# A fused S5 scan and sliding-window attention kernel rebuilt around frames of two steps, with rotation matrices on VectorE and GpSimd left idle

## The chip, the cores and the metric

The kernel runs on one core of a Trainium2 chip. The core has five engines that run side by side and meet through semaphores: PE (TensorE, the matrix engine), DVE (VectorE), ACT (ScalarE), POOL (GpSimd) and SP (SyncE, which issues most of the transfers here). PEld is PE's weight load, which overlaps PE. SBUF is the on-chip memory; PSUM holds what PE produces, and copying a PSUM tile to SBUF is called an eviction here.

The metric is device time in microseconds (us); lower is better. A ratio is the mean time of one kernel's fast runs over that of the kernel before in the same rounds on the same chip, so it is not quite the ratio of the medians quoted beside it. Where I write a difference in microseconds between two variants, it is the difference of their ratios times 212.0 us, a typical median of the kernel before in these rounds. A compile-time scheduler re-sorts each engine's instructions after every edit, so I do not read effects below about 1% (2 us) as causes unless the trace shows them too.

## The reference

Two independent parts run over 2048 positions of width 448 in bf16; the result is their concatenation, 2048 x 896.

```python
# Part A: S5, a diagonal complex recurrence with 448 states
dt = exp(log_dt); Lam_bar = exp(dt * Lam)                 # Lam = Lambda_re + i Lambda_im
B_bar = ((Lam_bar - 1) / Lam)[:, None] * (B_re + 1j*B_im)
h[t] = Lam_bar * h[t-1] + B_bar @ x[t]
y[t] = 2 * Re(C @ h[t]) + Dskip * x[t]

# Part B: attention, 16 heads of 28, window of 8 keys, dilation 2
q, k, v = split(x @ wqkv)
logits[s, w] = q[s] . k[s - 2w] / sqrt(28)     # -1e9 where s - 2w < 0
o[s] = sum_w softmax_w(logits)[s, w] * v[s - 2w]
out = o @ wo
```

Both kernels put 128 chunks of 16 consecutive positions on the 128 partitions, so that "position j" means 128 rows, one from each chunk. Attention needs 14 positions of the chunk before: the halo, which is copied by DMA; the first chunk's halo is zero. PE makes the projections. The logits and the weighted sum of v are elementwise products and sums on VectorE, because each position has its own keys. In part A, multiplying a state by a power of Lam_bar is a 2x2 rotation, which PE applies as a sparse 128x128 "rotation matrix"; these are built on the chip from the parameters.

## The kernel before

The order of the calls is: B's projections, A's weights and scan, then B's attention last.

```python
    b.prep(); a.setup(); b.qk_proj(); b.v_proj()
    a.setup_c(); a.setup_weights(); b.loads2()
    a.main()
    b.attention()
```

`prep` loads x whole, permutes the qkv weights with VectorE copies, and fills the first halo with zeros by DMA:

```python
        nc.sync.dma_start(self.x_sb[:], self.B_x[0].rearrange("(p j) d -> p j d", j=T))
        # ... (prep)
        V.tensor_copy(wpv[:, :, 0:2], wnv[:, :, 0:2])
        V.tensor_copy(wpv[:, :, 2], wnv[:, :, 2])
        # ... 16 transposes of x_sb, evicted by ScalarE
        nc.sync.dma_start(t_[0:1, :, 0:HALO, :]...)      # zeros, for kd and vd
```

The logits and the product with v use one temporary each (`qd`, `kd`, `vd` hold all 16 positions):

```python
        for w in range(W):                        # attention
            V.tensor_tensor(pr[:], qd[:]..., kd[:, :, off:off + T, :]..., op=ALU.mult)
            V.tensor_tensor(pr[:, 0:14], pr[:, 0:14], pr[:, 14:28], op=ALU.add)
            # ... four more halvings, the last into fp32 logits
        # ... softmax in fp32
        for (j0, j1) in self.PV_SPLIT:            # ((0, 12), (12, 16))
            for w in range(W):
                # ...
                tmp = pool.tile([NCH, DH, T, H], bf16, name="pv_tmp", tag="prod")   # one buffer
                V.tensor_tensor(tmp[:, :, 0:n, :], aa, vv, op=ALU.mult)
                V.tensor_tensor(acc[:, :, j0:j1, :], acc[:, :, j0:j1, :], tmp[:, :, 0:n, :], op=ALU.add)
            self.tail(j0, j1)       # transpose, VectorE eviction, wo product, ScalarE eviction, store
```

Part A builds its matrices on GpSimd (`build_mats(..., G)`), steps through 16 positions, and sends every local state through DRAM and back (`hs`) until the carried-in state is known:

```python
        for j in range(T):
            ht = self._level1_step(j, (lambda m: prev_t[:, m, :]), j > 0)   # 128-column products
            nc.sync.dma_start(hs[j], ht[:]...)
        # ... seven scan steps over the 128 chunks
        for j in range(T):
            nc.sync.dma_start(hin[:]..., hs[j])
            # ... hin + rotation of the carried-in state; then y = C h + Dskip x
```

## Time and profile before

The kernel before takes 211.73 us (median of 3 runs, 211.53 to 213.08). The profiled run spans 211.4 us.

| what | before | view |
|---|---|---|
| VectorE busy | 181.0 us, 86% | page, part 1 |
| PE busy | 160.4 us, 76% | page, part 1 |
| PE columns streamed | 335,040, about 141 us at 448 columns per 0.189 us | counted from the matmul records |
| first product on PE | 18.5 us | list of waits |
| VectorE idle in the first 20 us | 11.1 us | table by stretches |
| VectorE idle from there to its last instruction | 14.5 us | table by stretches and timeline |
| after VectorE's last instruction | 4.8 us | timeline |

These are lines of the page of the kernel before: the busy time of each engine with its share and its instructions; the busy tenths of PE and VectorE in 40 slices of 5.3 us; and the shares of the chain of work that ended last.

```profile
PE 160.4 (76%) x1709; PEld 117.4 (56%) x1709; DVE 181.0 (86%) x197; ACT 100.2 (47%) x193; POOL 28.1 (13%) x35
PE   0004999999997799999995763998888883297773
DVE  0359998888929999999999996999999999999950
PE 46%; DVE 33%; ACT 8%; DMA 6%; issue 3%; SPq 2%; ACTq 0%; DVEq 0%
```

VectorE is busy from slice 4 to slice 38, with dips at slices 12 and 25. PE does nothing for three slices, and it has holes while attention ends the kernel. One line of the list of waits says why nothing starts (waiter, its tile, what released it, us in total, times, longest):

```profile
PE pt_x L80 <- DMA xb_sb<-in_B_x_dram: 18.5, 1, 18.5
```

The table by stretches gives, after the stretch and its length, the busy us and the instructions of PE, PEld, DVE, ACT and POOL, then PE's clock, the DMA share and GB/s. Before:

```profile
0.00:20.00 20.00, 1.22 (x10) 1.12 (x11) 8.90 (x30) 5.37 (x12) 1.15 (x19) 1.00 0.66 184
110.00:141.00 31.00, 21.02 (x238) 15.68 (x236) 28.07 (x27) 19.74 (x36) 0.00 (x0) 0.89 0.16 49
141.00:204.00 63.00, 46.77 (x413) 30.05 (x412) 61.68 (x43) 23.77 (x49) 0.00 (x0) 0.92 0.28 83
```

In the last of these stretches VectorE is busy for 61.68 us of 63: there the kernel waits for VectorE. The groups by shape show what it does (line, engine, operation, output and input, shape and type, count, busy us, mean ns, idle before); the last one is a GpSimd matrix:

```profile
L129 DVE TENSOR_TENSOR prod<-qd,kd 128x7168 bf16<-128x7168 bf16 x8 | 30.7, 3840 | 0.1
L165 DVE TENSOR_TENSOR pv_tmp<-attn,vd 128x5376 bf16<-128x5376 bf16 x7 | 20.7, 2957 | 0.2
L167 DVE TENSOR_TENSOR acc<-acc,pv_tmp 128x5376 bf16<-128x5376 bf16 x6 | 17.7, 2957 | 0.2
L343 POOL TENSOR_TENSOR Mmat<-Dm,Scat 128x896 bf16<-128x896 f32 x7 | 11.6, 1688 | 19.3 <-DVE Scat L335 19.3
```

Two pairs from the timeline (start, length, engine, line, operation): in the first, a copy of 7 elements in each partition lasts as long as the GpSimd product beside it; in the second, a product and its sum follow one another.

```profile
23.26 3.19 POOL L343 TENSOR_TENSOR Lmat<-Dm,Shl 128x1792 bf16<-128x1792 f32 x1 [0.61 <-DVE Shl L340]
23.30 3.17 DVE L327 COPY sB<-g_im 64x7 f32<-64x7 f32 x1
...
147.73 2.96 DVE L165 TENSOR_TENSOR pv_tmp<-attn,vd 128x5376 bf16<-128x5376 bf16 x1
150.72 2.96 DVE L167 TENSOR_TENSOR acc<-acc,pv_tmp 128x5376 bf16<-128x5376 bf16 x1
```

### The profile page before, as it was taken

To read this page: it belongs to the slowest core of one execution; us is meant where nothing else is said; L and a number is where in the kernel's file an instruction comes from. 1 tells how busy PE (TensorE), PEld (TensorE's weight loads), DVE (VectorE), ACT (ScalarE), POOL (GpSimd) and SP (SyncE) were. 2 spreads that over 40 slices of the span, in tenths; PEclk is the share of its full clock that TensorE was granted. 3 is DMA by queue.
4 is the path that set the end of the run, shared out by engine and by line. 5 is a ranking of instruction groups with operands and counts; after the bars stand their busy time and mean duration, and the time that the engine had idled before them with its cause. 6 is when DMAs were issued, how large, how long until landed. Compare 5 with 4: busy or idle time off the path is not lost.

```text
span 211.4 us, 4117 instructions
## 1 busy us (share of the span) xinstructions
PE 160.4 (76%) x1709; PEld 117.4 (56%) x1709; DVE 181.0 (86%) x197; ACT 100.2 (47%) x193; POOL 28.1 (13%) x35
## 2 busy tenths in 40 slices
PE   0004999999997799999995763998888883297773
PEld 0003765555567799999994652565555551154441
DVE  0359998888929999999999996999999999999950
ACT  2053792002689993344337796344455541024432
POOL 2000899991000000000000000000000000000000
PEclk9999999999999999999999998599999999569999
DMA  1599940485508515422231011134354411012212
GB/s 0 103 351 289 244 108 0 108 192 161 212 2 209 95 47 171 164 106 90 87 118 59 3 43 43 47 110 129 92 137 126 112 43 43 0 43 72 83 65 87
DMA packets 23836, 22.17 MB, mean 105 GB/s; under 512 B 11786, under 2 KB 23114, under 8 KB 23562
## 3 DMA queue, kind: packets, MB, share of 16 engines
q1 hardware_dynamic: 20231, 20.32, 32.9%
q10 hardware_dynamic: 3587, 1.59, 3.2%
q8 instruction: 13, 0.21, 0.5%
q14 instruction: 5, 0.04, 0.1%
HBM read 11.36 MB, written 7.34 MB: 88 GB/s over the span
## 4 chain that ended last, share of the span: by engine, by line
PE 46%; DVE 33%; ACT 8%; DMA 6%; issue 3%; SPq 2%; ACTq 0%; DVEq 0%
PE qkv_ps L95 18%; DVE pv_tmp L165 13%; DVE acc L167 10%; PE l1A L392 7%; DMA xb_sb<-in_B_x_dram 6%; PE l1B L392 5%; PE wo_ps L188 3%; PE pt_x L80 3%; DVE oT_sb L185 2%; PE pt_x L415 2%; DVE o_nat L169 2%; ACT Bcat L379 2%; PE l1A L397 1%; PE l1A L399 1%; ACT Ccat L250 1%
## 5 line engine op out<-in xcount | busy, mean ns | idle before, releaser
L95 PE MATMUL qkv_ps<-wqkv_p,xbT_sb 112*128 112x448 bf16 x192 | 40.1, 361 | 0.0
L129 DVE TENSOR_TENSOR prod<-qd,kd 128x7168 bf16<-128x7168 bf16 x8 | 30.7, 3840 | 0.1
L165 DVE TENSOR_TENSOR pv_tmp<-attn,vd 128x5376 bf16<-128x5376 bf16 (+1 forms) x14 | 28.3, 2021 | 0.3
L95 PEld LDWEIGHTS <-xbT_sb 112*128 112x128 bf16 x192 | 18.8, 100 | 15.5
L392 PEld LDWEIGHTS <-Bcat 112*128 112x128 bf16 x448 | 26.2, 98 | 0.0
L167 DVE TENSOR_TENSOR acc<-acc,pv_tmp 128x5376 bf16<-128x5376 bf16 (+1 forms) x12 | 24.3, 2024 | 0.3
L80 PE MATMUL pt_x<-ident,xb_sb 128*112 128x128 bf16 x64 | 7.8, 266 | 18.8 <-DMA xb_sb<-in_B_x_dram 18.5
L483 ACT CAST ya<-y_ps 128x448 bf16<-128x448 f32 x16 | 8.5, 531 | 23.4 <-issue 18.8
L191 ACT CAST yb<-wo_ps 128x448 bf16<-128x448 f32 x16 | 8.5, 532 | 23.3 <-PE wo_ps L188 23.3
L80 PEld LDWEIGHTS <-xb_sb 128*112 128x112 bf16 x64 | 7.5, 173 | 21.1 <-DMA xb_sb<-in_B_x_dram 18.5
L402 ACT CAST ht<-l1A 128x512 bf16<-128x512 f32 x16 | 9.4, 587 | 19.2 <-issue 17.0
L119 ACT CAST vd<-qkv_ps 128x448 bf16<-128x448 f32 x16 | 8.4, 536 | 20.8 <-PE qkv_ps L95 20.7
L392 PE MATMUL l1A<-xaT_sb,Bcat 112*128 112x128 bf16 x256 | 18.1, 219 | 0.0
L188 PE MATMUL wo_ps<-wo_p,oT_sb 112*128 112x448 bf16 x64 | 15.0, 382 | 3.8 <-DVE oT_sb L185 3.7
L131 DVE TENSOR_TENSOR prod<-prod 128x3584 bf16<-128x3584 bf16 x8 | 16.2, 2025 | 0.3
L343 POOL TENSOR_TENSOR Mmat<-Dm,Scat 128x896 bf16<-128x896 f32 x7 | 11.6, 1688 | 19.3 <-DVE Scat L335 19.3
L392 PE MATMUL l1B<-xaT_sb,Bcat 112*128 112x128 bf16 x192 | 14.2, 219 | 0.0
L81 ACT COPY xbT_sb<-pt_x 112x512 bf16<-112x512 bf16 x16 | 8.8, 587 | 7.3 <-PE pt_x L80 7.3
L184 PE MATMUL pt_o<-ident,o_nat 128*112 128x128 bf16 x64 | 5.8, 244 | 8.3 <-DVE o_nat L169 8.3
L113 DVE TENSOR_SCALAR qd<-qkv_ps 128x448 bf16<-128x448 f32 x16 | 10.0, 625 | 2.1
L188 PEld LDWEIGHTS <-oT_sb 112*128 112x128 bf16 x64 | 6.0, 103 | 10.1 <-DVE oT_sb L185 5.0
L469 PEld LDWEIGHTS <-ident 128*128 128x128 bf16 x112 | 11.3, 101 | 0.0
(206 smaller groups left out, 360.9 us busy)
## 6 DMA issues: line engine op xcount, KB each, us to landing
hs<-ht SPq DMA_DIRECT2D x16, 224.0 KB, 1.9
hin<-hs SPq DMA_DIRECT2D x16, 224.0 KB, 2.7
xb_sb<-in_B_x_dram SPq DMA_DIRECT2D x1, 1792.0 KB, 12.3
xa_sb<-in_A_x_dram SPq DMA_DIRECT2D x1, 1792.0 KB, 7.9
out_dram<-ya SPq DMA_DIRECT2D x16, 112.0 KB, 1.7
out_dram<-yb SPq DMA_DIRECT2D x16, 112.0 KB, 1.7
kd<-kd ACTq DMA_DIRECT2D x1, 1372.0 KB, 9.1
vd<-vd SPq DMA_DIRECT2D x1, 1372.0 KB, 9.4
```

Source lines behind the costliest of these rows:

```text
L80: nc.tensor.transpose(pt[:, k, :], self.x_sb[:, j, k * KP:(k + 1) * KP], self.ident[:])
L95: nc.tensor.matmul(ps[:].rearrange("p d h -> p (d h)"), lhsT=self.xT[:, k, j, :], rhs=self.wp[:, k * 3 + which].rearrange("p d h -> p (d h)"),
L113: V.tensor_scalar(self.qd[:, :, j, :], ps[:], scale, None, op0=ALU.mult)
L129: V.tensor_tensor(pr[:], qd[:].rearrange("p d j h -> p d (j h)"), kd[:, :, off:off + T, :].rearrange("p d j h -> p d (j h)"), op=ALU.mult)
L131: V.tensor_tensor(pr[:, 0:14], pr[:, 0:14], pr[:, 14:28], op=ALU.add)
L165: V.tensor_tensor(tmp[:, :, 0:n, :], aa, vv, op=ALU.mult)
L167: V.tensor_tensor(acc[:, :, j0:j1, :], acc[:, :, j0:j1, :], tmp[:, :, 0:n, :], op=ALU.add)
L188: nc.tensor.matmul(ps[:], lhsT=oT[:, kt, j, :], rhs=self.wo_p[:, kt, :], start=(kt == 0), stop=(kt == KT - 1))
L343: eng.tensor_tensor(out_tile, Dm[:].unsqueeze(1).unsqueeze(1).to_broadcast([NCH, n, 2, PL]), scal.unsqueeze(3).to_broadcast([NCH, n, 2, PL ...
L392: nc.tensor.matmul(reg(m), lhsT=self.Bcat[:, k, m, :], rhs=self.xT[:, k, j, :], start=(k == 0 and m in (0, MA)), stop=(not has_prev and k ...
L402: nc.scalar.copy(ht[:, 0:MA, :], psA[:])
L469: nc.tensor.matmul(reg(m), lhsT=ident[:], rhs=hin[:, m, :], start=(m in (0, MA)), stop=False, skip_group_check=True)
```

## The change

The intent is to take work off VectorE, to keep PE fed from the start to the end, and to keep GpSimd out of VectorE's way. Nearly every line is rewritten, so the diff is cut to its core here, in the order of the kernel, with "..." at the cuts and comments of mine.

```diff
+    def warm(self, n, mode="full"):            # products of zeros while PE would wait
+            if mode == "full":
+                mm(wp[0][:, 0:NCH], lhsT=z[:, 0:NCH], rhs=z[:, 0:NCH], start=True, stop=True)
+            elif mode == "cols":                # 32 columns of the array at a time
+            else:                               # "rows": 64 rows of the array at a time
 ...
-        nc.sync.dma_start(self.x_sb[:], self.B_x[0].rearrange("(p j) d -> p j d", j=T))
+        self.nc.sync.dma_start(self.x_sb[:, j0:j1, :], xv[:, j0:j1, :])     # five pieces, w in thirds
-        V.tensor_copy(wpv[:, :, 0:2], wnv[:, :, 0:2])
-        V.tensor_copy(wpv[:, :, 2], wnv[:, :, 2])
+        pv = ps[:].rearrange("p (h d) -> p d h", h=H)      # the permutation is done by the eviction
 ...
-        for w in range(W):                                  # logits: all 16 positions, one prod buffer
+    def qk(self, hf):                                       # logits: 8 positions, two pr buffers
+            V.tensor_tensor(pr[:].rearrange("p d j h -> p j d h"), self.q[hf][:], self.kd[:, off:off + HJ], op=ALU.mult)
+            V.tensor_tensor(pr[:, 0:14], pr[:, 0:14], pr[:, 14:28], op=ALU.add)
+            V.tensor_tensor(pr[:, 0:7], pr[:, 0:7], pr[:, 7:14], op=ALU.add)
+            V.tensor_tensor(pr[:, 0:3], pr[:, 0:3], pr[:, 4:7], op=ALU.add)
+            for d in range(4):                              # the last adds on PE
+                nc.tensor.matmul(lgs[w // 4][:, w % 4, :], lhsT=cx.ident[:], rhs=pr[:, d]..., ...)
 ...
-    PV_SPLIT = ((0, 12), (12, 16))
-                    tmp = pool.tile([NCH, DH, T, H], bf16, name="pv_tmp", tag="prod")
+    def pv(self, hf, at, jl0, jl1):                         # 4 positions at a time
+            self.pvb = pool.tile([NCH, 7, 4, DH, H], bf16, name="pvb", tag="kd")
+        acc = self.pvb[:, self.acci]                        # 3 sums in turn
+            t_ = self.pvb[:, 3 + self.pvi] if w else acc    # 4 temporaries in turn
+                self.pvi = (self.pvi + 1) % 4
 ...
-            nc.vector.tensor_copy(oT[:, :, j, :], pt[:])
+        nc.scalar.copy(oT[:], pt[:])
 ...
-            build_mats(self.Mmat[:, s_ * NM:(s_ + 1) * NM], Scat[:, 6 + s_], NM, G)    # G = gpsimd
+        nc, G, ident = self.nc, self.nc.vector, self.cx.ident                          # G = vector
+        for i in range(1, 5):
+            self.mat(KPOW[i], Scat[:, i], G)
+        for i in range(5, NPW):                                                        # scan_mats
+            self.mat(KPOW[i], self.Scat[:, i], self.nc.vector)
 ...
-        for j in range(T):                                  # level 1: 16 steps, hs to DRAM and back
-            eng.dma_start(hs[j], ht[:].rearrange("p m c -> p (m c)"))
+        for e in range(2):                                  # level 1: frames of two, 512 columns
+            for m in range(NM):
+                        nc.tensor.matmul(ps[:], lhsT=self.Bcat[:, b, k, m, :],
+                                         rhs=self.xT[2 * e + b][:, k]..., ...)
 ...
+    def rot_c(self, eng):       # two rotated C: one for odd positions, one with which even ones read the odd state before
+    def make_k0(self, eng):     # K0 = B C + Dskip: the newest x goes straight to y
 ...
+            for _ in range(2):
+                next(fill, None)            # rot_c and K0 fill the waits between scan steps
```

The states are kept for the odd positions only; y at an even position comes from the state of the position before, through a rotated C, and from its own x through `K0`. The seven scan matrices, the six others of `params_g` and the first are 14 products of 896 elements, all on VectorE. The calls are interleaved: B's k and q, logits of the second half, logits of the first half, v and A's weights, then VectorE's products with v beside A's level 1, scan and y on PE.

The halo zeros were already written by DMA in the kernel before; "by DMA" is new only against a version that fills them on GpSimd, which is run as an experiment below.

## The prediction

> **What bounds the kernel now.** VectorE. The page gives it 181.0 us busy of 211.4 (86%), against PE 160.4 and ScalarE 100.2. The table by stretches has it busy 41.6 of 42.0 us from 141 to 183 us and 29.2 of 30.0 from 80 to 110 us. Its 30 us of idleness lie at the two ends: the first 20 us hold only 8.9 us of VectorE work, because the first transpose waits 18.5 us for the whole of xb_sb (list of waits), and after the last product-sum at 202.9 us come 8.5 us of tail (transpose, wo product, eviction, store).
>
> **VectorE before, from the groups by shape:** logits 69 us (of it L129 30.7, L131 16.2, L132 8.7), softmax 11, probability times V 61, evictions and weight permutation 35, small parameter work about 9 of which 5 to 6 are three tiny copies that took 1.6 to 3.2 us beside a GpSimd product.
>
> **VectorE after, from the same durations** (128x3584 bf16 2.02 us, 1792 1.09, 768 0.56, 256 0.29; so about 157 ns plus 0.52 ns per bf16 element; f32 products 1024 elements 1.23):
> - logits: per offset and half 2.02+1.09+0.62+0.36 = 4.1 us, x16 = 65 us; the last adds go to PE as accumulating identity products.
> - probability times V: 60 operations of 1792 elements at 1.09 = 65 us.
> - softmax in bf16, with subtraction and sum on PE: 5 us.
> - evictions: 14 instead of 48, 8 us.
> - rotation matrices: 14 of 896 f32 elements at about 1.1 us (estimate) = 15 us, new on VectorE. (GpSimd: 1.69 each, off the critical path). Parameter work 8 us.
> Sum 166 us, only 15 less than now.
>
> **The ends.** x arrives in pieces and w by thirds, so PE starts near 5 us and the halves' first q and k are ready near 13 us (estimate: about 1.7 MB at the 250 to 350 GB/s of slices 3 to 5). I expect about 6 us idle at the start, 6 us of gaps and softmax waits, and 8 us of tail, now with both evictions on ScalarE. 166+6+6+8 = 186; I take 185.
>
> **Other engines.** PE must stream about 345,000 columns, as many as now; at 189 ns per 448 columns (134 qkv matmuls in 25.35 us) that is 145 us. Level 1 and the y products shrink, K0, rot_c and Gt are new, and the DRAM round trip of hs (about 7 MB) goes. ScalarE grows to about 124 us (206 evictions near 0.56 us, table loads). PE should finish part A near 165 us, hidden by VectorE, but with little to spare.
>
> The column- and row-tiled warm-up runs while PE would wait for data: worth under 1 us. The Trainium skill ("TensorE: Matmul & The Clock Gate", The HAM clock gate) says activity releases the throttle; here the first transposes took 266 ns against 217 later, which agrees, but VectorE isn't bound by that.
>
> **Predicted 185 us, 80% range 174 to 196; faster by over 2% 0.95, within 2% 0.04, slower 0.01.**
>
> **Right if:** VectorE busy 160 to 172 us at 88 to 92% of the span; matrices 1.0 to 1.2 us each; products of 1792 elements still near 1.09 us; first logits product before 18 us; idle VectorE about 20 us; GpSimd busy under 3 us; chain of waits mostly VectorE.
>
> **Wrong if:** short inner runs of 16 elements halve VectorE's rate (1792 elements at 1.9 us: far slower); PE or ScalarE finish part A after VectorE (PE's fixed order, three mm banks, scan steps of 1.3 us), adding 5 to 15 us; or the start is faster than I think (175).

## The result, and the profile after

| | before | after |
|---|---|---|
| median (range), us | 211.73 (211.53 to 213.08) | 177.65 (176.85 to 177.68) |
| ratio, 95% interval | | 0.8349 (0.8298 to 0.8400) |
| span of the profiled run, us | 211.4 | 175.9 |
| VectorE: sum of the lengths of its records, us | 186.5 | 166.5 |
| VectorE busy (records that overlap counted once), us | 181.0 | 151.7 |
| end of VectorE's last instruction, us | 206.6 | 160.7 |
| PE busy, us | 160.4 | 163.7 |
| PE columns (15,360 of the warm-up left out, three missing records counted) | 335,040 | 342,425 |
| HBM read and written, MB | 11.36, 7.34 | 6.89, 3.67 |

The result is correct. The same lines of the page after:

```profile
PE 163.7 (93%) x1215; PEld 95.6 (54%) x1218; DVE 151.7 (86%) x210; ACT 109.7 (62%) x216; POOL 2.6 (1%) x25
PE   7986998989999999999999989999999999998992
DVE  1469999999999999999979999999999999995000
DVE 55%; PE 30%; ACT 9%; issue 4%; ACTq 0%; DVEq 0%
```

PE now works from the first slice to the last. VectorE starts earlier, has one small dip (slice 21), and does nothing in the last three slices; in the kernel before it was busy nearly to the last slice. Note that PE's busy share rose from 76% to 93% at nearly the same number of columns (7% more with those of the warm-up). The Trainium skill ("Trainium Kernel Development and Optimization", Performance Expectations) calls matmul busy time a bad metric, so I count streamed columns instead: 448 columns take 0.188 to 0.189 us back to back, or 2.4 per ns, and 342,425 columns make about 143 us.

The stretches after (columns as above):

```profile
0.00:20.00 20.00, 16.94 (x138) 10.09 (x139) 12.05 (x44) 9.29 (x19) 2.63 (x25) 1.00 1.02 212
110.00:160.00 50.00, 48.91 (x350) 28.64 (x348) 49.97 (x51) 30.73 (x63) 0.00 (x0) 1.00 0.17 54
160.00:167.00 7.00, 6.27 (x44) 3.38 (x44) 0.73 (x1) 4.61 (x9) 0.00 (x0) 1.00 0.20 66
167.00:175.90 8.90, 5.63 (x30) 2.70 (x28) 0.00 (x0) 1.60 (x3) 0.00 (x0) 1.00 0.20 64
```

From 110 to 160 us PE and VectorE are both full. After 160.7 us VectorE has nothing, and PE and ScalarE work on for 15 us. Counted as streamed columns at 2.4 per ns, PE uses 8.2 to 9.2 us in every 10 from 20 to 60 us, 8.0 to 9.2 from 60 to 100, only 6.7 from 100 to 110 (the scan), and 8.5 to 9.5 from 110 to 160. The kernel before had 4.5 to 5.3 in every 10 from 110 to 140 us.

The groups by shape after:

```profile
L210 DVE TENSOR_TENSOR pvb<-attn,vd 128x1792 bf16<-128x1792 bf16 x32 | 34.1, 1082 | 0.0
L156 DVE TENSOR_TENSOR pr<-q,kd 128x3584 bf16<-128x3584 bf16 x16 | 31.7, 2014 | 0.9 <-PE lg L162 0.9
L213 DVE TENSOR_TENSOR pvb<-pvb 128x1792 bf16<-128x1792 bf16 x28 | 30.2, 1080 | 0.0
L381 DVE TENSOR_TENSOR mat<-Dm,Scat 128x896 bf16<-128x896 f32 x12 | 13.0, 1082 | 0.0
```

Lengths are as predicted: 1.08 us for 1792 elements although the innermost run is 16 elements, 2.01 us for 3584, 1.08 us for a matrix. But the timeline shows that the steps are shorter than the lengths. Three neighbours in the product with v:

```profile
111.42 1.08 DVE L213 TENSOR_TENSOR pvb<-pvb 128x1792 bf16<-128x1792 bf16 x1
112.43 1.08 DVE L210 TENSOR_TENSOR pvb<-attn,vd 128x1792 bf16<-128x1792 bf16 x1
113.43 1.08 DVE L213 TENSOR_TENSOR pvb<-pvb 128x1792 bf16<-128x1792 bf16 x1
```

They start 1.00 us apart and last 1.08: the next one starts 0.08 us before the record of the last one ends. This is what the four temporaries bought.

The end of the kernel, from the timeline:

```profile
158.53 2.21 DVE L213 TENSOR_TENSOR pvb<-pvb 128x1792 bf16<-128x1792 bf16 x2
...
166.46 0.53 ACT L230 CAST yb<-wo_ps 128x448 bf16<-128x448 f32 x1 [0.23 <-PE wo_ps L228]
...
170.38 0.92 PE L546 MATMUL y_ps<-K,xaT 112*128 112x448 bf16 x4
171.14 1.49 PE L550 MATMUL y_ps<-Ccat,h 128*128 128x448 bf16 x7
172.71 0.53 ACT L553 CAST ya<-y_ps 128x448 bf16<-128x448 f32 x1 [1.55 <-PE y_ps L550]
```

VectorE ends at 160.7. What follows from it (transpose, wo product, eviction `yb`) is done at 166.99. Part A's last eviction `ya` is done at 173.24. So VectorE's path has 173.24 - 166.99 = 6.2 us of slack, and PE's y products end the kernel, although the chain of waits above gives VectorE 55% and PE 30%. The list of waits says the same from ScalarE's side:

```profile
ACT ya L553 <- PE y_ps L550: 17.6, 14, 1.6
```

**Where the 35.5 us of span went.** Cut at the first 20 us and at VectorE's last instruction, the span is VectorE's busy time plus its idle times: VectorE's busy time fell by 29.3 us (20.0 because the sum of its records fell from 186.5 to 166.5, and 9.3 because the overlap of records rose from 5.5 to 14.8); its idle time in the first 20 us fell by 3.1 (11.1 to 8.0); its idle time in the middle fell by 13.4 (14.5 to 1.1); and the time after its last instruction rose by 10.4 (4.8 to 15.1). That is -29.3 - 3.1 - 13.4 + 10.4 = -35.4. This is bookkeeping and not a test: it says where the time went, and the experiments below undo only parts of the change. No run undoes the new order of the calls, the loads in pieces, the evictions that left VectorE or the last adds on PE, so how much each of these is worth is not shown.

### The profile page after: what moved, and what is told of

Same layout as the page of the kernel before. It is cut to its first block, busy times and chain, and to the rows that moved or that the text cites. A ratio compares the mean times of both kernels' runs of the same rounds, so it can differ in the third digit from the quotient of the medians.

```text
span 175.9 us, 3127 instructions
## 1 busy us (share of the span) xinstructions
PE 163.7 (93%) x1215; PEld 95.6 (54%) x1218; DVE 151.7 (86%) x210; ACT 109.7 (62%) x216; POOL 2.6 (1%) x25
## 3 DMA queue, kind: packets, MB, share of 16 engines
HBM read 6.89 MB, written 3.67 MB: 60 GB/s over the span
## 4 chain that ended last, share of the span: by engine, by line
DVE 55%; PE 30%; ACT 9%; issue 4%; ACTq 0%; DVEq 0%
DVE pvb L210 18%; DVE pvb L213 16%; PE l L453 9%; DVE pr L156 6%; PE qkv_ps L138 5%; ACT xaT L80 4%; DVE mat L381 4%; DVE pr L157 3%; PE y_ps L550 3%; PE wo_ps L228 2%; DVE pr L158 2%; DVE q L88 2%; PE lg L162 2%; PE pt_b L398 2%; PE warm L65 2%
## 5 line engine op out<-in xcount | busy, mean ns | idle before, releaser
L138 PE MATMUL qkv_ps<-wqkv_nat,xbT 112*128 112x448 bf16 x192 | 40.1, 352 | 2.1 <-DVE xbT L86 1.1
L210 DVE TENSOR_TENSOR pvb<-attn,vd 128x1792 bf16<-128x1792 bf16 x32 | 34.1, 1082 | 0.0
L156 DVE TENSOR_TENSOR pr<-q,kd 128x3584 bf16<-128x3584 bf16 x16 | 31.7, 2014 | 0.9 <-PE lg L162 0.9
L213 DVE TENSOR_TENSOR pvb<-pvb 128x1792 bf16<-128x1792 bf16 x28 | 30.2, 1080 | 0.0
L453 PE MATMUL l<-xaT,Bcat 112*128 112x512 bf16 x112 | 28.3, 379 | 0.2
L138 PEld LDWEIGHTS <-xbT 112*128 112x128 bf16 x192 | 17.8, 98 | 16.6 <-DVE xbT L86 1.5
L157 DVE TENSOR_TENSOR pr<-pr 128x1792 bf16<-128x1792 bf16 x16 | 16.7, 1080 | 0.0
L453 PEld LDWEIGHTS <-Bcat 112*128 112x128 bf16 x112 | 10.5, 97 | 10.5 <-issue 0.2
L228 PE MATMUL wo_ps<-wo_p,oT 112*128 112x448 bf16 x64 | 13.5, 354 | 0.3
L381 DVE TENSOR_TENSOR mat<-Dm,Scat 128x896 bf16<-128x896 f32 x12 | 13.0, 1082 | 0.0
```

Source lines behind the costliest of these rows:

```text
L138: nc.tensor.matmul(ps[:], lhsT=self.xT[j // 4][:, k, j % 4, :], rhs=self.wn[:, k, which, :], start=(k == 0), stop=(k == KT - 1))
L156: V.tensor_tensor(pr[:].rearrange("p d j h -> p j d h"), self.q[hf][:], self.kd[:, off:off + HJ], op=ALU.mult)
L210: V.tensor_tensor(t_[:, 0:n], at[:, w, jl0:jl1, :].unsqueeze(2).to_broadcast([NCH, n, DH, H]), self.vd[:, off:off + n], op=ALU.mult)
L213: V.tensor_tensor(acc[:, 0:n], acc[:, 0:n], t_[:, 0:n], op=ALU.add)
L228: nc.tensor.matmul(ps[:], lhsT=oT[:, kt, :], rhs=self.wo_p[:, kt, :], start=(kt == 0), stop=(kt == KT - 1))
L381: eng.tensor_tensor(t_[:], self.Dm[:].unsqueeze(1).unsqueeze(1).to_broadcast([NCH, NM, 2, PL]), scal.unsqueeze(3).to_broadcast([NCH, NM, 2 ...
```

## The experiments

Two theories stand against each other. **Theory P**: the kernel after is ended by PE's stream, part A's y products; VectorE's path has 6.2 us of slack, and work on VectorE costs little until that is used up. **Theory V**, the prediction's: VectorE ends the kernel, as the chain of waits suggests with its 55%. Besides, three claims need a test: that temporaries in turn give real overlap, that GpSimd must be idle, and that the warm-up is worth little.

The last column is against the kernel after, as described. The interval of the kernel after itself is about 1.1 us either way. All but the two marked ones passed the comparison with the reference.

| run | median us | ratio to before, 95% | us against after |
|---|---|---|---|
| after | 177.65 | 0.8349 (0.8298 to 0.8400) | |
| pv_onebuf | 178.80 | 0.8406 (0.8369 to 0.8443) | +1.2 |
| y_noskip (wrong) | 171.38 | 0.8055 (0.8015 to 0.8095) | -6.2 |
| few_mats | 176.50 | 0.8307 (0.8261 to 0.8354) | -0.9 |
| both_cut (wrong) | 168.98 | 0.7957 (0.7931 to 0.7982) | -8.3 |
| g_all | 186.65 | 0.8782 (0.8746 to 0.8819) | +9.2 |
| g_early | 182.98 | 0.8633 (0.8579 to 0.8687) | +6.0 |
| g_scan | 184.36 | 0.8691 (0.8651 to 0.8732) | +7.3 |
| halo_pool (its three fast runs) | 181.52 | 0.8534 (0.8470 to 0.8598) | +3.9 |
| plain_warm | 177.24 | 0.8349 (0.8324 to 0.8374) | 0.0 |
| no_warm | 179.06 | 0.8444 (0.8412 to 0.8477) | +2.0 |
| rot_l1 | 179.53 | 0.8458 (0.8423 to 0.8493) | +2.3 |
| rot_l1c | 179.57 | 0.8458 (0.8414 to 0.8502) | +2.3 |

### One temporary in the product with v (pv_onebuf)

```diff
-                self.pvi = (self.pvi + 1) % 4
+                self.pvi = 0
```

> One temporary buffer instead of four for the products of probability and V, so each add follows the product it reads and each product follows the add that frees the buffer. Theory A (independent neighbours overlap on VectorE): the step from one 1792-element operation to the next goes from 1.00 us to about 1.11, that is about 6 us more for the 60 of them. Rival (the overlap of the records is only bookkeeping): the step stays at 1.00 us. If VectorE alone sets the time, the whole kernel takes 5 to 6 us longer (183 us); if the stream of PE sets it, under 2 us longer.

The timeline of pv_onebuf at the same place, and its last evictions:

```profile
112.21 1.09 DVE L213 TENSOR_TENSOR pvb<-pvb 128x1792 bf16<-128x1792 bf16 x1
113.34 1.09 DVE L210 TENSOR_TENSOR pvb<-attn,vd 128x1792 bf16<-128x1792 bf16 x1
114.46 1.09 DVE L213 TENSOR_TENSOR pvb<-pvb 128x1792 bf16<-128x1792 bf16 x1
...
171.99 0.53 ACT L230 CAST yb<-wo_ps 128x448 bf16<-128x448 f32 x1 [0.23 <-PE wo_ps L228]
173.65 0.53 ACT L553 CAST ya<-y_ps 128x448 bf16<-128x448 f32 x1 [1.13 <-PE y_ps L550]
```

With each product overwriting the temporary that the sum before it reads, the step is 1.126 us (median) in place of 1.002. So the overlap is real, not an artefact of how ends are recorded: VectorE's last instruction ends at 166.3 us in place of 160.7, 5.6 us later. The kernel, however, is only 1.2 us slower, which its interval hardly tells from nothing. The last `yb` now ends at about 172.5 us and the last `ya` at about 174.2: VectorE's delay has been eaten by its slack. That is theory P's picture; under theory V most of the 5.6 us should have shown.

The Trainium skill ("VectorE: DVE Perf Modes", The DRAIN you can't avoid) says that the next operation does not start until the pipe is empty, and adds that one which is not held starts earlier. The trace of the kernel after agrees with the addition: a neighbour starts 0.08 us before the record of the one before ends. The same page's section "Rules for kernel authors" advises to minimise the number of operations; the number of operations with v rose from 30 to 60, at the same number of elements, and independence between them was worth 5.6 us, so independence counts as well.

### Less work on PE, on VectorE, and on both (y_noskip, few_mats, both_cut)

y_noskip leaves out x's share of y: 17,920 fewer columns on PE, or 7.5 us at 2.4 per ns. Its result is wrong (relative error 0.132).

```diff
-        for k in range(KT):
+        for k in range(0):
             x_ = self.xT[b][:, k, a, :]
 ...
-            nc.tensor.matmul(ps[:], lhsT=l_, rhs=self.C[:, 1 - b % 2, m, :], start=False, stop=(m == NM - 1),
+            nc.tensor.matmul(ps[:], lhsT=l_, rhs=self.C[:, 1 - b % 2, m, :], start=(m == 0), stop=(m == NM - 1),
```

> Wrong result on purpose: the products of x with K0 and Dg in y are left out, 17,920 columns of PE, 7.5 us at full clock; VectorE's work and order are untouched. If VectorE sets the time: at most 2 us faster, through a less crowded tail. If PE's stream sets it: 5 to 7.5 us faster. If both bind (PE until VectorE's end plus its tail): about 4 us, down to VectorE's last result at 160 us plus 8 us of tail plus 3.

few_mats builds none of the seven scan matrices and uses one of the others in their place: 6.1 us less VectorE work. It is not the function that was asked for, but its error stays within the comparison's tolerance; it is a probe, not a version to use.

```diff
-            self.mat(KPOW[i], self.Scat[:, i], self.nc.vector)
+            self.mats[KPOW[i]] = self.mats[12]
```

> Wrong result on purpose: the seven matrices of the long scan are not made, one of the others stands in for them; VectorE loses 7 x 1.0 us, PE's work is untouched. If VectorE sets the time: 6 to 7 us faster (about 170.5). If PE's stream sets it: under 2 us faster, and PE ends near 170 us as before.

both_cut makes both edits, and is wrong in the same way as y_noskip.

> Wrong result on purpose: both cuts together, 7.5 us of PE stream and 7 matrices of VectorE. PE's cut alone gave 6 us, VectorE's alone 1.2. If the two engines bind in turn (PE up to where VectorE's last result plus its tail stands), the sum exceeds its parts: VectorE ends near 154.6, its tail of 8 to 9 us ends near 164, and the time is 9 to 11 us below the changed kernel (about 167). If PE alone binds throughout: about 7 us below (170.5).

The end of y_noskip in the timeline:

```profile
158.49 2.21 DVE L213 TENSOR_TENSOR pvb<-pvb 128x1792 bf16<-128x1792 bf16 x2
...
166.43 0.53 ACT L230 CAST yb<-wo_ps 128x448 bf16<-128x448 f32 x1 [0.22 <-PE wo_ps L228]
```

VectorE ends at 160.7 us, exactly as in the kernel after, with its instructions in the same order; nothing changed for it. Yet the kernel is 6.2 us faster, and the last work is now `yb` at 166.96. PE lost 7.5 us, and the kernel gained just the 6.2 us of slack before VectorE's tail ended last.

The end of few_mats:

```profile
152.39 2.21 DVE L213 TENSOR_TENSOR pvb<-pvb 128x1792 bf16<-128x1792 bf16 x2
...
170.96 0.53 ACT L553 CAST ya<-y_ps 128x448 bf16<-128x448 f32 x1 [1.55 <-PE y_ps L550]
```

Here VectorE ends 6.1 us sooner, at 154.6, and the kernel gains 0.9 us, within the noise of the two. The trace shows the last `ya` ending at 171.5 against 173.2, so a little of VectorE's time does reach PE; I suppose through the wo products, which then come sooner and leave PE free later, but no run tests that. both_cut gains 8.3 us: VectorE ends at 155.5, the last `yb` at 161.8 and the last `ya` at 164.6, so PE ends last again. I had expected 9 to 11 us if the two engines bind in turn and about 7 if PE alone does; 8.3 lies between, so this run does not decide between the two. Its last evictions:

```profile
161.24 0.53 ACT L230 CAST yb<-wo_ps 128x448 bf16<-128x448 f32 x1 [0.23 <-PE wo_ps L228]
...
164.08 0.53 ACT L553 CAST ya<-y_ps 128x448 bf16<-128x448 f32 x1 [0.84 <-PE y_ps L550]
```

These four runs fit one number, the slack of 6.2 us. Taking 7.5 us from PE gains it all; taking 6.1 us from VectorE gains about 1; adding 5.6 us to VectorE costs about 1; taking from both gains more than either. Theory V, by which few_mats should have gained most of 6 us and y_noskip nothing, falls for the end of the kernel.

### Matrices on GpSimd (g_all, g_early, g_scan)

g_all puts 13 of the 14 matrices on GpSimd; g_early only the six of `params_g`; g_scan only the seven of `scan_mats`.

```diff
-            self.mat(KPOW[i], Scat[:, i], G)                          # g_all, g_early ("g", "gl" too)
+            self.mat(KPOW[i], Scat[:, i], nc.gpsimd)
-            self.mat(KPOW[i], self.Scat[:, i], self.nc.vector)        # g_all, g_scan
+            self.mat(KPOW[i], self.Scat[:, i], self.nc.gpsimd)
```

> 13 of the 14 rotation matrices on GpSimd, all but the first (undoes that part of the change). They cost VectorE 13 x 1.0 us of its time. If VectorE alone sets the time and nothing collides: 10 to 13 us faster (about 166 us), GpSimd busy about 22 us at 1.69 us each. If PE's stream sets it: 0 to 3 us faster. If GpSimd and VectorE get in each other's way on operations with two inputs from the same memory: VectorE's busy time stays near 152 us or rises, logits products of 2.01 us get longer beside GpSimd, and the time stays or rises.

> Six matrices (2, 4, 8, 12, g, gl) on GpSimd, the seven of the scan stay on VectorE. If the harm of the run with 13 came from GpSimd beside VectorE's tiny operations and evictions before the first logits product: most of its 9 us come back here (5 to 8 us slower than the changed kernel, first logits product after 33 us). If it came from the logits products: no slower than the changed kernel.

> Only the seven matrices of the scan on GpSimd. They run beside the logits products or just before. If any two-input VectorE operation beside a GpSimd product waits for it: the 7 x 1.0 us that VectorE saves are given back, 1.69 us for each; VectorE ends within 3 us of 160.7 and the time is within 2 us of the changed kernel, or up to 5 us above it if the evictions of k and q are held up. If they don't collide: VectorE ends near 154 us as with the seven left out, and the time is 1 to 2 us lower.

From the timeline of g_all:

```profile
13.22 9.13 POOL L381 TENSOR_TENSOR mat<-Dm,Scat 128x896 bf16<-128x896 f32 x5 [10.03 <-DVE Scat L326]
13.24 2.61 DVE L381 TENSOR_TENSOR mat<-Dm,Scat 128x896 bf16<-128x896 f32 x1
...
17.45 1.61 DVE L344 TENSOR_TENSOR g_re<-g_re,t 128x7 f32<-128x7 f32 x1
...
22.29 0.15 DVE L354 TENSOR_TENSOR gl_im<-g_re,pw_im 128x7 f32<-128x7 f32 x1
...
36.31 4.99 DVE L156 TENSOR_TENSOR pr<-q,kd 128x3584 bf16<-128x3584 bf16 x2
```

The same line of the kernel after, where the logits start:

```profile
29.38 2.02 DVE L156 TENSOR_TENSOR pr<-q,kd 128x3584 bf16<-128x3584 bf16 x1
```

While GpSimd multiplies, a VectorE matrix takes 2.61 us in place of 1.08, and an operation on 7 elements 1.61 us; where it falls at the end of the GpSimd products, the same sort of operation takes 0.15. The evictions from PSUM keep their 0.61 to 0.62 us, but they queue behind the held ones, PE waits for them, and the logits start 6.9 us later. PE's granted clock falls as well: the table by stretches gives 0.50 for 18.2 to 21.5 us and for 25.1 to 31.8 us, and 18 qkv products start 0.30 to 0.37 us apart in place of 0.189. This adds to the harm but is not the main part of it: the profiled run of g_early has a clock of 1.00 throughout and spans 5.1 us more than the kernel after all the same. The harm is done although VectorE's busy time fell (149.9 us against 151.7): moving 13 matrices off the "bottleneck" cost 9.2 us.

I had hoped that g_early and g_scan would part the harm done at the start from harm done beside the logits. They did not: in g_scan GpSimd ran its seven matrices at once, from 13.5 to 28.6 us, at a mean of 2.19 us each, not beside the logits. The first logits product came at 35.91 us in g_scan and 35.20 in g_early, and PE streamed 4.6 and 5.8 us in the 10 from 20 to 30 us, against 8.8 in the kernel after. Both pay by the same late start. g_scan's 7.3 us also lie outside what I had written down for it (within 2 us, or up to 5). The only sight of the conflict beside the logits is g_all's first logits product, which ran beside the last GpSimd matrix and took 3.05 us in place of 2.02; what it would cost there in all stays open.

The Trainium skill ("SBUF — State Buffer", SBUF: two separate sides) describes a port pair that VectorE and GpSimd share under a lock held for a whole instruction, taken by VectorE operations with two SBUF inputs only against a GpSimd operation that reads SBUF, and by its two-port modes against any. The trace agrees for the first kind: 0.15 us became 1.61, about one GpSimd matrix (1.69 us each in the kernel before).

### Halo zeros by GpSimd (halo_pool)

```diff
-        self.nc.sync.dma_start(t_[0:1, 0:HALO].rearrange("p j d h -> p j (d h)"),
-                               self.cx.wz[0:1, 0:D].unsqueeze(1).to_broadcast([1, HALO, D]))
+        self.nc.gpsimd.memset(t_[0:1, 0:HALO], 0.0)
```

> The halo zeros of k and v by GpSimd fills of one row instead of DMA (undoes that part of the change). Two fills of 6272 elements, by the 448-element fill at 0.47 us some 6 us each (estimate). No theory gives them weight: within 1% of the changed kernel; up to 2 us slower if VectorE's operations wait for the fills or the first k eviction waits for its zeros.

I had given this no weight, and missed: it costs 3.9 us, or 2.2%, over its three fast runs. The profiled run is the fastest of them and spans only 2.1 us more than the kernel after; the other two had a lower granted clock (0.972 against 0.990), and no trace of them was kept, so the rest of the 3.9 us is not explained. The two fills touch one partition only, but GpSimd needs 5.31 us for each, and this is what VectorE does beside the second:

```profile
7.57 5.31 POOL L124 MEMSET vd<- 1x6272 bf16 x1
7.94 0.25 DVE L302 TENSOR_TENSOR ang<-kv,at 128x84 f32<-128x84 f32 x1
8.44 4.50 DVE L303 TENSOR_SCALAR kf<-ang 128x84 f32<-128x84 f32 x1
```

The operation with two inputs is not held (0.25 us), the one with one input and constants is held for 4.50 us until the fill ends at 12.88. That is the other half of the statement in the skill's page: a fill reads nothing, so two-input operations pass, and an operation that can run in a two-port mode waits. The first logits product came at 33.64 us, 4.3 us late; here too PE's clock fell to 0.50, from 15.3 to 18.6 us. So "halo zeros by DMA" and "matrices on VectorE" are the same idea twice: leave GpSimd idle while VectorE prepares the start.

### The warm-up (plain_warm, no_warm)

plain_warm makes the column-tiled and row-tiled warm-up products plain ones; no_warm takes all four warm-ups out.

```diff
-    cx.warm(16)                 # no_warm: all four lines gone
-    cx.warm(12, "cols")         # plain_warm: cx.warm(12)
-    cx.warm(8, "rows")          # plain_warm: cx.warm(8)
 ...
-    cx.warm(24)
```

> The 20 column- and row-tiled warm-up products become plain 128x128 ones (20 x 0.056 to 0.11 us instead of 3.2 us of stream). Both theories: within 1% of the changed kernel, since PE has no data before 6.4 us. If the fill matters for the clock: the granted clock falls below 1.0 in the first 12 us and the first products take 1.5 to 2 times as long, at most 2 us in all.

> No warm-up product at all. If the clock gate counts: the first transposes and qkv products near 6.5 us run at half speed [...], PE ends 1.5 to 2.5 us later; as PE binds, the whole is that much longer (179). If warm-up is worthless: the same within 1%, or up to 1.3 us faster because the 24 products in the middle are gone.

plain_warm has the ratio of the kernel after (0.8349): the tiling of the warm-up products is worth nothing that these rounds can see. Having none costs 2.0 us against the kernel after and by the ratio of the same rounds the same against plain_warm; the two profiled spans differ by 1.1 us (177.0 against 175.9). The first 12 qkv products, first in the kernel after, then in no_warm:

```profile
8.43 2.44 PE L138 MATMUL qkv_ps<-wqkv_nat,xbT 112*128 112x448 bf16 x12
```

```profile
7.77 4.69 PE L138 MATMUL qkv_ps<-wqkv_nat,xbT 112*128 112x448 bf16 x12
```

And the first 10 us of no_warm in the table by stretches (columns as before):

```profile
0.00:10.00 10.00, 4.06 (x20) 2.56 (x21) 3.47 (x19) 4.30 (x9) 2.62 (x25) 1.00 0.83 257
```

Without the warm-up these products start 0.374 us apart until about 12 us, and 0.189 afterwards. The Trainium skill ("TensorE: Matmul & The Clock Gate", Part 1) says that an idle PE runs at half rate until activity releases the clock; 0.374 against 0.189 agrees. The column of PE's clock in the stretch, the number after POOL's, says 1.00 for the same time, but that is no record: the clock records kept with this trace begin only at 12.3 us, with full speed, just after the last slow product, which starts at 11.9 us, and the view gives 1.00 where it has none. In the kernel after they begin at 6.1 us. So the records and the steps agree here: the page has a caveat that such records can be unreliable, and this trace gives no case of it. The step between products shows the slow clock where the column does not.

### Two attempts to close PE's hole in the scan (rot_l1, rot_l1c)

If PE ends the kernel, the 3.3 us that it does not stream from 100 to 110 us (the scan) should be worth something. In rot_l1 the 14 products of `rot_c` run inside level 1, so that only K0 is left to fill the scan, one group in every second step; rot_l1c does it in level 1's second half only, two for each group.

```diff
-    def level1(self):
+    def level1(self, fill):
 ...
                 nc.scalar.copy(self.h[:, e, m, :], ps[:])
+                next(fill, None)                    # rot_l1c: for _ in range(2 * e): next(fill, None)
 ...
-            for _ in range(2):
+            if s_ % 2 == 0:
                 next(fill, None)
 ...
-    a.level1()
-    a.scan(itertools.chain(a.rot_c("A"), a.make_k0("A")))
+    a.level1(a.rot_c("A"))
+    a.scan(a.make_k0("A"))
```

> A try for a faster version, result correct: the 14 products that rotate C and their evictions move from the scan into level 1, where ScalarE is busy 7 of 20 us, and the scan is filled with the four K0 groups alone (28 products, 4 evictions). PE's stream is unchanged; the scan stretch from 100 to 110 us, where PE streams 6.7 us of 10, should gain 2 to 4 us. If PE's stream with its holes sets the time: 2 to 4 us faster (about 174.5). If not: no change.

> Correct. As rot_l1, but the C rotations go only between the seven groups of level 1's second half (two after each), so that none takes a PSUM bank while ScalarE's transposes hold level 1 back; rot_l1 gained about 2 us of PE stream at 100 to 110 us and lost 3 at 60 to 70. If PE's holes set the time: the hole at 60 to 70 us closes again (8 us of stream in 10) and the whole is 2 to 3 us below the changed kernel (175). If the time is set elsewhere: no change.

Both are 2.3 us slower, which neither of my two cases allowed for. In rot_l1 the stretch from 100 to 110 us did fill (8.4 us in 10 against 6.7), but 60 to 70 us emptied (5.0 against 8.0): as I read it, the new products took PSUM banks that level 1 had used to run ahead beside the transposes. What rot_l1c shows is that the hole goes when the products leave that place. rot_l1c closed that one (7.75), and lost in 80 to 100 us (8.5 and 7.9 against 9.2 and 8.3): PE waits 0.3 to 0.46 us for each group, because its eviction on ScalarE stands behind two of the new ones. ScalarE is what these tries ran into. I found no version faster than the kernel after; whether PE's holes can be closed stays open.

## Why the prediction was right or wrong

The verdict and the range were right: 185 us predicted, 174 to 196, and 177.65 measured. The centre was 7 us too slow, and the way to it had two wrong steps that partly cancel; that the number came so near is in part luck.

1. **"Sum 166 us", used as busy time: wrong.** The sum was right as a sum of lengths: the records add up to 166.5 us. Its main terms were right too (products of 1792 elements 1.08 us, matrices 1.08 us, no penalty for inner runs of 16). But I then added idle times to it as if records did not overlap, and tested it with "VectorE busy 160 to 172 us"; busy was 151.7. I had the right lengths from a kernel whose neighbours depend on each other (steps of 2.99 us at 2.96), and did not see that four temporaries would let them overlap. pv_onebuf measured it: 0.12 us for each operation, 5.6 us at VectorE's end.
2. **"PE should finish part A near 165 us, hidden by VectorE": wrong.** Part A's last y came out at 173.2 us; VectorE's own tail was done at 167.0. The term "8 us of tail" measured 15.1; for VectorE's own tail it was about right (8.9 us in y_noskip, where that tail ends the kernel). I had PE's stream right (145 us predicted, 143 counted) but took too little for the holes between its products: it streams 6.7 us in 10 in the scan and 8 to 9.5 elsewhere, and needs 173 us for 143. That PE might finish after VectorE stood under "Wrong if", at 5 to 15 us; it happened and cost 6.2, as y_noskip shows, while step 1 gave back 14.8.
3. **"about 6 us idle at the start, 6 us of gaps":** 8.0 and 1.1 measured. With the tail, 166.5 - 14.8 + 8.0 + 1.1 + 15.1 = 175.9, the span.
4. **"first logits product before 18 us": wrong**, 29.38 us. PE did start early, but before the logits VectorE had eight matrices, parameter work and evictions to do, and did them without idling from about 14 us on. I put the matrices in the sum and forgot that some stand in front of the logits. It does no harm to VectorE's sum, only to its order.
5. **"GpSimd: 1.69 each, off the critical path": wrong** in what it implies, that the matrices would be cheaper there. g_all costs 9.2 us, through the start. The "three tiny copies that took 1.6 to 3.2 us beside a GpSimd product" in the kernel before were the hint; I counted them as a saving and did not turn it round.
6. **"ScalarE grows to about 124 us":** 109.7. GpSimd under 3 us: 2.6, right. "Worth under 1 us" for the tiled warm-up: right for the tiling (nothing seen), while a warm-up of any kind is worth 1 to 2 us.
7. **"chain of waits mostly VectorE":** it is, 55%, so the sign that I had named for my theory was met while the theory was wrong about the end. The chain follows one path and says nothing about how close the next one is. It took runs that lighten one engine at a time to see that PE ends the kernel.

What stays open: whether PE's holes (the scan, and 60 to 80 us with ScalarE busy for 17.3 of 20) can be closed; what GpSimd would cost beside the logits alone; what the parts of the change that no run undoes are worth; and every difference below about 1%.

## What to carry to other kernels

Add up start-to-start steps of VectorE, not record lengths, and give neighbouring operations different buffers: independent neighbours of 1.08 us stepped at 1.00 us, dependent ones at 1.13. Before taking work off the engine that the chain of waits names, compare when the last result of each engine's path is done: here 6.1 us less VectorE work gained 0.9 us and 7.5 us less PE work gained 6.2. GpSimd work beside VectorE is not free because it is off the critical path: 13 matrices cost 9 us there and two one-row fills 2 to 4 us, both with a later start of the logits (by 6.9 and 4.3 us).

## What the Trainium skill lacked or had wrong

- "VectorE: DVE Perf Modes", The DRAIN you can't avoid: it says that an operation which is not held starts earlier, but gives no size there and none for a dependence between neighbours, and the rules at its end name only the number of operations. The runs show 1.002 us between independent operations of 1792 bf16 elements and 1.126 us between dependent ones, with records of 1.08 and 1.09 us; over the product with v this is 5.6 us.
- "SBUF — State Buffer": the shared lock is described rightly, but not what it does to tiny operations, which is where it hurt: 7 elements in 1.61 us in place of 0.15 beside a matrix on GpSimd, 84 elements in 4.50 us beside a fill of one partition, and GpSimd's own matrices at a mean of 2.2 us (g_scan) and 2.3 us (g_early) in place of 1.69.
- "GPSIMD Engine Reference": the cost of a fill of one partition is not there; 6,272 bf16 elements took 5.31 us.
